# Query and first MLP matrix loaded in one transfer each, as 4.5 rows a partition; 24 rows of the second MLP matrix in one transfer

## The chip, the core and the metric

The kernel runs on one core of a Trainium2 chip. A core has a matrix engine (TensorE, PE in the profile), a vector engine (VectorE, DVE), an activation engine (ScalarE, ACT), a general engine (GpSimd, POOL) and a sync engine (SyncE, SP) that here does little but issue transfers. Each runs its own instructions in program order and waits on semaphores; 16 DMA engines move data between HBM and the on-chip memory. The metric is the device time of one execution in microseconds (us).

## What is computed

One decode step, for a batch of 8 rows x of 576 numbers. Attention reads the last 2048 positions of a cache of 16 key and value heads (32 query heads, 128 wide); beside it an MLP of hidden size 4608 works on the layernormed x; a gate mixes the two.

```python
W = min(4096, max(256, Sk // 4))                  # 2048
q = (x @ wq).reshape(B, Sq, Hq, Dh)               # 576 x 4096
k, v = cache[:, :, Sk - W:, :], repeated for 2 query heads each
o = softmax(q @ k.T * Dh ** -0.5) @ v
a = o.reshape(B, Sq, Hq * Dh) @ wo                # 4096 x 576
y = layernorm(x)
b = gelu(y @ w1 + b1) @ w2 + b2                   # 576 x 4608, 4608 x 576
g = sigmoid((x * gate_w).sum(-1))
return g * a + (1 - g) * b
```

## The kernel before

Nearly all bytes are the cache: 32 transfers of 4 MB (16 of keys, K0 to K15, 16 of values, V0 to V15), each into one of four slots of a large buffer, `RAW`. The slots are taken in the order 1, 2, 0, 3, and the transfers are issued by SP in the order K0, K1, V0, K2, V1, K3, V2 and so on (`stream`, lines 587 to 600). SP issues a transfer when its slot is free (`load_item`, lines 620 to 627, the list `slot_free`): a slot that held keys is free when its last transpose is done (L691), one that held values when its product with the probabilities is done (L754, L186).

The weights of the start lie in slots too. The query matrix `A_wq` goes to slot 0 and the first MLP matrix `B_w1` to slot 3, with a small remainder behind it. So V0 (slot 0) waits for the query matmuls, `o_qp`, and K2 (slot 3) for the MLP matmuls, `o_hp` (line 603).

Rows of the two matrices: 576 = 512 + 64. The first 512 rows lie four to a partition; the last 64 are cut in halves by columns, one half row a partition, so that they fill 128 partitions as well. Each matrix comes in two transfers (lines 417 to 421). A matmul multiplies 128 partitions at once, so there are five steps t over the rows: four for the main part, one for the remainder. The batch is only 8 wide, so four column quarters c of the matrix are multiplied side by side in four 32-column groups of the array (`held_x`, L497 to L505): in step t, a quarter of the output takes 2 matmuls of 512 columns (query) or 3 of 384 (MLP). That makes 5 x 4 x 2 = 40 and 5 x 4 x 3 = 60 matmuls. Those of one step that share their weights follow without a new weight load (line 175).

The transposed input (`xT`, `yT`) has one 128 x 8 block per step. `tr_in` (L448) makes four blocks straight from x with a column step of 4, and two from `xz` (or `yz`), where the last 64 columns are spread to every second place with zeros between, once for each half; `ev_T` copies all six from PSUM in one instruction (L462). DVE also makes the gate (L429, L430), the layernorm (L432 to L439, with a power on POOL, L438) and small masks before the query matmuls.

After the query matmuls: copy (L517), transpose (L522), selection matmuls (L528), four copies on ACT (L537), the mask of the scores (L874). After the MLP matmuls: gelu on ACT and DVE (L556 to L563). Then each key item n takes four transposes on DVE (L691), each followed by 8 matmuls (L709, L175), a maximum (L642), an exponential (L648) and the mask of the next item (L652).

At the end come the bias, the first 24 of 36 rows of `B_w2` in two transfers of 12 (`M_CUTS`, L599), the output matrix in four, and the last 12 rows of `B_w2` in 8, 3 and 1 (`m2_chunk`, L852).

No order is written by hand: a planner, `_Plan.schedule` (L62), orders each engine's work by costs given with each operation.

Of the kernel before, what the change touches and what calls it, by code (L numbers as in the profile page):

```python
# [192 lines left out]
def build_kernel(nc, A_x, A_k_cache, A_v_cache, A_wq, A_wo, B_x, B_w1, B_b1, B_w2, B_b2, gate_w, out):  # L193
# [16 lines left out]
    FCW = 32 * FT  # L210
    HN = 3
    HW_ = FCW // HN
    QCW = Hq * Dh // FC
# [8 lines left out]
    with ExitStack() as es:  # L222
# [34 lines left out]
        req("cols", 16, F32)  # L257
        req("xT", 6 * 32, BF)
        req("yT", 6 * 32, BF)
        req("q4", 4 * 256, BF)  # L260
# [24 lines left out]
        over("y_bf", "PT", 2304, D, BF)  # L285
        over("xz", "PT", 3456, 256, BF)
        over("yz", "PT", 3968, 256, BF)
        over("b1c", "PT", 4608, FCW, BF)
# [37 lines left out]
        cols = view("cols")  # L326
        xT = view("xT").rearrange("p (t b) -> p t b", b=32)
        yT = view("yT").rearrange("p (t b) -> p t b", b=32)
        q4 = view("q4").rearrange("p (h m) -> p h m", h=4)
# [23 lines left out]
        x_sb, gw_sb, y_bf = view("x_sb", 8), view("gw_sb", 8), view("y_bf", 8)  # L353
        xz = view("xz", 8).rearrange("p (s c) -> p s c", s=2)
        yz = view("yz", 8).rearrange("p (s c) -> p s c", s=2)
        xg, xc, sq = view("xg", 8), view("xc", 8), view("sq", 8)
# [4 lines left out]

        wq_m = RAW[:, 0:4 * 4096].rearrange("p (t c) -> p t c", t=4)
        W1O = (ND - 1) * DE
        WQR = W1O + 4 * F + F // 2
        wq_r = RAW[:, WQR:WQR + 2048]
        w1_m = RAW[:, W1O:W1O + 4 * F].rearrange("p (t c) -> p t c", t=4)
        w1_r = RAW[:, W1O + 4 * F:W1O + 4 * F + F // 2]

# [27 lines left out]
        o_nhalf = add("pool", lambda e: e.memset(col(C_NHALF, 8), -0.5), name="nhalf", cost=0.1)  # L396
        o_xz0 = add("pool", lambda e: e.memset(view("xz", 8), 0.0), name="xz0", cost=0.2)
        o_yz0 = add("pool", lambda e: e.memset(view("yz", 8), 0.0), name="yz0", cost=0.2)
        o_z = add("pool", lambda e: e.memset(zeros_bf, 0.0), name="zeros", cost=0.15)
# [16 lines left out]
        db = [d_b1]  # L416
        d_wqr = dma("sp", lambda e: e.dma_start(wq_r, A_wq[512:576, :].rearrange("k (s c) -> (k s) c", s=2)), "wq", 64 * 8192, name="d_wqr")
        d_wqm = dma("sp", lambda e: e.dma_start(wq_m.rearrange("p t c -> p (t c)"), A_wq[0:512, :].rearrange("(p t) c -> p (t c)", t=4)), "wq", 512 * 8192, name="d_wqm", after=[d_wqr])
        dwq = [d_wqm, d_wqr]
        d_w1m = dma("sp", lambda e: e.dma_start(w1_m.rearrange("p t c -> p (t c)"), B_w1[0:512, :].rearrange("(p t) c -> p (t c)", t=4)), "w1", 512 * F * 2, name="d_w1m", after=[d_wqm])  # L420
        d_w1r = dma("sp", lambda e: e.dma_start(w1_r, B_w1[512:576, :].rearrange("k (s c) -> (k s) c", s=2)), "w1", 64 * F * 2, name="d_w1r", after=[d_w1m])
        dw1 = [d_w1m, d_w1r]


        o_xz = []
        for s in range(2):
            o_xz.append(add("dve", (lambda s=s: lambda e: e.tensor_copy(xz[:, s, :].rearrange("p (k z) -> p k z", z=2)[:, :, s], x_sb[:, 512:576]))(),  # L427
                            deps=dx + [o_xz0], name="xz%d" % s, cost=0.12))
        o_xg = add("dve", lambda e: e.tensor_tensor(out=xg, in0=x_sb, in1=gw_sb, op=ALU.mult), deps=dx, name="xg", cost=0.7)  # L429
# [9 lines left out]
        o_y = add("dve", lambda e: e.tensor_scalar(out=y_bf, in0=xc, scalar1=col(C_RSTD, 8), scalar2=None, op0=ALU.mult), deps=[o_rstd, o_xc], name="y", cost=0.4)  # L439
        o_yz = []  # L440
        for s in range(2):
            o_yz.append(add("dve", (lambda s=s: lambda e: e.tensor_copy(yz[:, s, :].rearrange("p (k z) -> p k z", z=2)[:, :, s], y_bf[:, 512:576]))(),
                            deps=[o_y, o_yz0], name="yz%d" % s, cost=0.12))
# [4 lines left out]
        def tr_in(name, z, which):  # L448
            def fn(e):
                ins = None  # L450
                for t in range(4):
                    src = bass.AP(arena, offset=aoffs(name) + t, ap=[[AST, 8], [4, 128]])
                    ins = e.transpose(ps_bf[:, BK_X, which * 64 + t * 8: which * 64 + t * 8 + 8], src, ident[0:8, 0:8])  # L453
                for s in range(2):
# [10 lines left out]
        o_gp = add("pe", lambda e: e.matmul(ps[:, BK_X, 400:402], r8, cols[0:8, C_G:C_G + 2], start=True, stop=True), deps=[o_g, o_omg, o_r8], name="g_pe", cost=0.4, after=[o_yTp])  # L465
        o_yT = add("dve", ev_T(yT, 1), deps=[o_gp, o_yTp, o_yT0], name="yT_ev", cost=0.2)
        o_gcol = add("dve", lambda e: e.tensor_copy(gcol, ps[:, BK_X, 400:401]), deps=[o_gp], name="gcol_ev", cost=0.15)
# [134 lines left out]
        last_dma = [d_w1r]  # L602
        slot_free = [[o_qp], [], [], [o_hp]]
# [248 lines left out]
        def m2_chunk(ci):  # L852
# [95 lines left out]
```

## Time and profile before

| | us |
|---|---|
| median of 3 runs | 364.70 (364.68 to 364.73) |
| the profiled execution, its own time | 364.7 |
| span of the profile, first to last instruction | 363.4 |
| busy: PE, DVE, ACT, POOL | 274.3, 253.9, 131.6, 76.0 |
| moved by DMA | 154.45 MB, mean 425 GB/s |
| mean granted TensorE clock | 0.944 |

The profile page gives busy time by engine, the span in 40 slices, DMA queues, the chain of work that ended last, and groups of instructions by line. Beside the page the trace can be asked for a timeline, for stretches (windows) and for each transfer's time from issue to landing. In a line of the timeline stand the start in us, the length, the engine and line, the operation, what it writes and reads, and how many instructions were merged; in brackets how long its engine had been idle and who released it. A busy TensorE counts pipelined matmuls, so its busy time is no measure of its load.

| issue to landing of the first transfers | issued, us | landed after, us |
|---|---|---|
| query, last 64 rows in halves, 512 KB | 0.81 | 3.4 |
| query, 512 rows, 4096 KB | 1.25 | 12.9 |
| MLP, 512 rows, 4608 KB | 1.72 | 23.4 |
| MLP, last 64 rows in halves, 576 KB | 2.19 | 24.3 |
| K0 | 2.7 | 34.6 |
| V0 | 20.41 | 36.2 |
| K2 | 32.81 | 33.4 |

### The profile page before, as it was taken

What the parts mean: (1) busy time and instruction counts of PE and PEld (TensorE: products, weight loads), DVE (VectorE), ACT (ScalarE), POOL (GpSimd) and SP (SyncE); (2) the same over time, 40 slices, a digit from 0 to 9 for tenths busy, and PEclk for the clock granted to TensorE, in tenths of its full rate; (3) what the DMA queues carried; (4) which work ended last, traced back from release to release, by engine and by line L of the source; (5) the groups of instructions that cost most, each with busy time, mean ns of one, the idle gap of its engine ahead of it and who ended that gap; (6) DMA issues with size and microseconds to landing.
All of it is one profiled execution on the core that took longest, in us unless ns stands there. A gap on an engine that the chain in (4) does not pass through costs nothing.

```text
span 363.4 us, 4421 instructions
## 1 busy us (share of the span) xinstructions
PE 274.3 (75%) x1830; PEld 125.7 (35%) x1382; DVE 253.9 (70%) x196; ACT 131.6 (36%) x117; POOL 76.0 (21%) x76
## 2 busy tenths in 40 slices
PE   0356454999897868895968869786879679988996
PEld 0110000345270605260524316251617034523763
DVE  0722978797978596939486778767695959498520
ACT  1012106274644443543333334444444407313300
POOL 9124001221414040403212040404040403003000
PEclk9975596999999999999999989999989969999999
DMA  8999999999999999999999999999999999999996
GB/s 349 433 422 420 447 418 448 415 451 418 451 415 453 411 458 408 453 411 454 413 451 415 451 415 451 415 451 413 451 418 447 418 447 416 449 418 434 416 425 251
DMA packets 6578, 154.45 MB, mean 425 GB/s; under 512 B 764, under 2 KB 932, under 8 KB 1320
## 3 DMA queue, kind: packets, MB, share of 16 engines
q1 hardware_dynamic: 6512, 154.29, 98.7%
q8 instruction: 6, 0.10, 0.1%
q10 hardware_dynamic: 56, 0.03, 0.0%
q14 instruction: 4, 0.03, 0.0%
HBM read 154.31 MB, written 0.01 MB: 425 GB/s over the span
## 4 chain that ended last, share of the span: by engine, by line
DMA 50%; DVE 33%; PE 9%; issue 4%; ACT 2%; ACTq 0%; POOL 0%; SPq 0%
DMA arena<-in_A_k_cache_dram 43%; DVE arena L691 20%; DMA arena<-in_B_w_dram 5%; DVE arena L666 5%; PE ps L175 4%; DMA arena<-in_gate_w_dram 2%; DVE arena L642 2%; PE ps L186 2%; DVE arena L800 1%; PE ps L502 1%; PE ps L709 1%; DVE arena L797 1%; DVE arena L563 1%; DVE arena L741 1%; ACT arena L648 1%
## 5 line engine op out<-in xcount | busy, mean ns | idle before, releaser
L691 DVE STREAM_TRANSPOSE arena<-arena 128x2048 f32<-128x2048 f32 x64 | 145.0, 2287 | 30.1 <-DMA arena<-in_A_k_cache_dram 28.4
L175 PE MATMUL ps<-arena 128*128 128x512 bf16 (+2 forms) x458 | 127.1, 428 | 11.4 <-DVE arena L691 8.7
L186 PE MATMUL ps<-arena 128*128 x942 | 105.5, 273 | 0.1
L741 POOL COPY arena<-arena 32x2048 bf16<-32x2048 bf16 x28 | 52.7, 1884 | 207.6 <-DVE arena L666 206.8
L186 PEld LDWEIGHTS ps<-arena 128*128 x942 | 91.9, 98 | 11.3 <-issue 0.6
L709 PE MATMUL ps<-arena 128*128 128x512 bf16 x120 | 48.9, 408 | 54.3 <-DVE arena L691 47.6
L740 ACT ACTIVATE arena<-arena 32x2048 bf16<-32x2048 bf16 x30 | 57.2, 1906 | 72.0 <-DVE arena L666 71.7
L709 PEld LDWEIGHTS ps<-arena 128*128 128x128 bf16 x128 | 13.1, 102 | 163.9 <-DVE arena L691 108.6
L648 ACT ACTIVATE arena<-ps,arena 128x2048 bf16<-128x2048 f32 x16 | 31.5, 1967 | 105.2 <-DVE arena L646 72.4
L642 DVE TENSOR_REDUCE arena<-ps 128x1 f32<-128x2048 f32 x16 | 36.7, 2291 | 30.9 <-PE ps L175 30.9
L666 DVE STREAM_TRANSPOSE arena<-arena 128x2048 bf16<-128x2048 bf16 x16 | 36.4, 2274 | 2.1 <-ACT arena L648 2.1
L652 ACT ACTIVATE ps<-arena 128x2048 f32<-128x2048 f32 x15 | 28.1, 1872 | 0.1
L754 PE MATMUL ps<-arena 128*128 128x256 bf16 x82 | 14.3, 272 | 1.0 <-DVE arena L741 1.0
L754 PEld LDWEIGHTS ps<-arena 128*128 128x128 bf16 x82 | 7.8, 98 | 16.1 <-issue 13.7
L453 PE MATMUL ps<-arena 8*128 8x8 bf16 x8 | 0.6, 171 | 14.7 <-DVE arena L427 9.6
L580 PE MATMUL ps<-arena 128*8 128x288 bf16 (+1 forms) x140 | 9.4, 286 | 1.4 <-DMA arena<-in_A_wo_dram 0.7
L558 DVE TENSOR_TENSOR arena<-arena 128x1152 f32<-128x1152 f32 x1 | 1.4, 1358 | 11.1 <-ACT arena L556 11.1
L724 POOL MEMSET arena<- 128x4096 f32 x1 | 3.5, 3511 | 22.6 <-DVE arena L741 22.6
L580 PEld LDWEIGHTS ps<-arena 128*8 128x8 bf16 (+1 forms) x140 | 5.8, 86 | 5.6 <-DMA arena<-in_B_w_dram 1.8
L635 POOL COPY arena<-arena 32x128 bf16<-32x128 bf16 x16 | 4.6, 287 | 14.5 <-ACT arena L537 7.8
L427 DVE COPY arena<-arena 8x64 bf16<-8x64 bf16 x2 | 0.3, 190 | 9.2 <-DMA arena<-in_gate_w_dram 9.2
L891 DVE CAST arena<-ps 8x288 bf16<-8x288 f32 x1 | 0.4, 446 | 8.6 <-PE ps L580 8.6
(104 smaller groups left out, 99.4 us busy)
## 6 DMA issues: line engine op xcount, KB each, us to landing
arena<-in_A_k_cache_dram SPq DMA_DIRECT2D x16, 4096.0 KB, 27.2
arena<-in_A_v_cache_dram SPq DMA_DIRECT2D x16, 4096.0 KB, 27.1
arena<-in_B_w_dram SPq DMA_DIRECT2D x1, 4608.0 KB, 23.4
arena<-in_A_wo_dram SPq DMA_DIRECT2D x4, 1152.0 KB, 22.5
arena<-in_A_wq_dram SPq DMA_DIRECT2D x1, 4096.0 KB, 12.9
arena<-in_B_w_dram SPq DMA_DIRECT2D x2, 1728.0 KB, 23.9
arena<-in_B_w_dram SPq DMA_DIRECT2D x1, 1152.0 KB, 19.8
arena<-in_B_w_dram SPq DMA_DIRECT2D x1, 576.0 KB, 24.3
```

What stands on the lines that cost most here:

```text
L175: return e.add_instruction(mybir.InstMatmult(name=nc.get_next_instruction_name(), engine=mybir.EngineType.PE, ins=[e.lower_ap(rhs), e.lowe ...
L186: return e.add_instruction(mybir.InstMatmult(name=nc.get_next_instruction_name(), engine=mybir.EngineType.PE, ins=[operand(r, r_ap), opera ...
L580: ins = e.matmul(ps[32 * j:32 * j + 8, BK_ACC, 0:JN], lhsT, rhs[:, JN * j:JN * j + JN], start=False, stop=True, skip_group_check=True, til ...
L642: mx = mx_done[n] = add("dve", lambda e: e.tensor_reduce(out=k(n, MX), in_=ps[:, 0:4, :].rearrange("p a n -> p (a n)"), axis=AXL.X, op=ALU ...
L648: ex = add("act", lambda e: e.activation(out=Pm, in_=ps[:, 0:4, :].rearrange("p a n -> p (a n)"), func=ACTF.Exp, bias=k(n, NB), scale=SCAL ...
L652: mask_done[n + 1] = add("act", lambda e: e.activation(out=ps[:, 0:4, :].rearrange("p a (n c) -> p (a n) c", c=32), in_=bass.AP(arena_f, o ...
L666: pt_done[n] = add("dve", lambda e: e.transpose(bass.AP(arena, offset=aoffs("PT") + 2048 * (n % 2), ap=[[AST, 128], [1, 2048]]), Pm), deps ...
L691: tr = add("dve", (lambda rh=rh, hh=hh, kb=kb: lambda e: e.transpose(bass.AP(arena_f, offset=foffs("KT") + kb * 2048, ap=[[AST // 2, 128], ...
L709: mm = e.matmul(*args, start=False, stop=True, skip_group_check=True) if rc == 0 else held_matmul(nc, e, *args, stop=True, skip=True)
L740: return e.activation(out=dst, in_=src, func=ACTF.Copy)
L741: return e.tensor_copy(dst, src)
L754: mm = e.matmul(ps[:, ob_, 0:256], lhsT, rhs, start=(k == 0), stop=True, skip_group_check=True)
```

## The change

The two matrices are seen as 1152 half rows of 2048 (query) or 2304 (MLP) columns. Partition p holds half rows 9p to 9p + 8, which lie together in HBM, so that one transfer of 36,864 or 41,472 bytes a partition loads a whole matrix. The query matrix now begins 4096 bytes ahead of slot 0, in the end of the buffer `KT`, and the MLP matrix ends behind slot 3, in the zone of `ptx0`.

A step i now takes the i-th half row of each partition. For even p + i that is a left half, for odd p + i a right half, of row (9p + i) // 2. So the input of a step is spread over the partitions (`rows_of`: two strided copies of 8 x 640, one for even and one for odd steps), transposed (nine transposes for each of x and y), and written to `xT` or `yT` twice, once masked by even and once by odd parity (`ev_T`: a product with the columns of `par`, two instructions each). The column quarters 0 and 1 use the blocks masked for left halves, 2 and 3 those for right halves. There are nine steps in place of five: 72 matmuls for 40 (query) and 108 for 60 (MLP). `xr` is shared by x and y, so the copies of y wait for the transposes of x. `par` is two small instructions on DVE from the identity matrix; the zeroed `xz` and `yz` and the four copies into them are gone, and the memsets of `xT` and `yT` on POOL cover 576 elements in place of 192.

The first 24 rows of `B_w2` come in one transfer. Their matmuls stay in two groups of 12, in the same order, both waiting for that transfer.

```diff
+    HR = 2 * D // 128
...
-        wq_m = RAW[:, 0:4 * 4096].rearrange("p (t c) -> p t c", t=4)
-        W1O = (ND - 1) * DE
-        WQR = W1O + 4 * F + F // 2
-        wq_r = RAW[:, WQR:WQR + 2048]
-        w1_m = RAW[:, W1O:W1O + 4 * F].rearrange("p (t c) -> p t c", t=4)
-        w1_r = RAW[:, W1O + 4 * F:W1O + 4 * F + F // 2]
+        QH, FH = Hq * Dh // 2, F // 2
+        WQO, W1O = aoffs("RAW") - (HR * QH - DE), aoffs("RAW") + (ND - 1) * DE
+        assert WQO >= aoffs("KT") + 6144 and W1O + HR * FH <= PX + SE
+        wq_sb = arena[:, WQO:WQO + HR * QH].rearrange("p (i c) -> p i c", i=HR)
+        w1_sb = arena[:, W1O:W1O + HR * FH].rearrange("p (i c) -> p i c", i=HR)
...
-        d_wqr = dma("sp", lambda e: e.dma_start(wq_r, A_wq[512:576, :].rearrange("k (s c) -> (k s) c", s=2)), "wq", 64 * 8192, name="d_wqr")
-        d_wqm = dma("sp", lambda e: e.dma_start(wq_m.rearrange("p t c -> p (t c)"), A_wq[0:512, :].rearrange("(p t) c -> p (t c)", t=4)), "wq", 512 * 8192, name="d_wqm", after=[d_wqr])
-        dwq = [d_wqm, d_wqr]
-        d_w1m = dma("sp", lambda e: e.dma_start(w1_m.rearrange("p t c -> p (t c)"), B_w1[0:512, :].rearrange("(p t) c -> p (t c)", t=4)), "w1", 512 * F * 2, name="d_w1m", after=[d_wqm])
-        d_w1r = dma("sp", lambda e: e.dma_start(w1_r, B_w1[512:576, :].rearrange("k (s c) -> (k s) c", s=2)), "w1", 64 * F * 2, name="d_w1r", after=[d_w1m])
-        dw1 = [d_w1m, d_w1r]
-
-
-        o_xz = []
-        for s in range(2):
-            o_xz.append(add("dve", (lambda s=s: lambda e: e.tensor_copy(xz[:, s, :].rearrange("p (k z) -> p k z", z=2)[:, :, s], x_sb[:, 512:576]))(),
-                            deps=dx + [o_xz0], name="xz%d" % s, cost=0.12))
+        half_rows = lambda w: w.rearrange("k (s c) -> (k s) c", s=2).rearrange("(p i) c -> p (i c)", i=HR)
+        d_wq = dma("sp", lambda e: e.dma_start(wq_sb.rearrange("p i c -> p (i c)"), half_rows(A_wq)), "wq", D * 8192, name="d_wq")
+        d_w1 = dma("sp", lambda e: e.dma_start(w1_sb.rearrange("p i c -> p (i c)"), half_rows(B_w1)), "w1", D * F * 2, name="d_w1", after=[d_wq])
+        dwq, dw1 = [d_wq], [d_w1]
...
+        o_par01 = add("dve", lambda e: e.tensor_reduce(out=par[:, 0:2], in_=ident.rearrange("p (k h) -> p h k", h=2), axis=AXL.X, op=ALU.add), deps=[o_ident], name="par01", cost=0.3, prio=1)
+        o_par = add("dve", lambda e: e.tensor_copy(par[:, 2:3], par[:, 0:1]), deps=[o_par01], name="par2", cost=0.12, prio=1)
+
+        def rows_of(name, odd):
+            def fn(e):
+                dst = bass.AP(arena, offset=aoffs("xr") + 128 - 127 * odd, ap=[[AST, 8], [256, (HR + 1) // 2], [128, 2], [2, 64]])
+                src = bass.AP(arena, offset=aoffs(name) + HR // 2 * odd, ap=[[AST, 8], [1, (HR + 1) // 2], [0, 2], [HR, 64]])
+                return e.tensor_copy(dst, src)
+            return fn
+
+        def tr_in(which):
             def fn(e):
                 ins = None
-                for t in range(4):
-                    src = bass.AP(arena, offset=aoffs(name) + t, ap=[[AST, 8], [4, 128]])
-                    ins = e.transpose(ps_bf[:, BK_X, which * 64 + t * 8: which * 64 + t * 8 + 8], src, ident[0:8, 0:8])
-                for s in range(2):
-                    ins = e.transpose(ps_bf[:, BK_X, which * 64 + 32 + s * 8: which * 64 + 40 + s * 8], z[:, s, :], ident[0:8, 0:8])
+                for i in range(HR):
+                    ins = e.transpose(ps_bf[:, BK_X, which * 128 + i * 8: which * 128 + i * 8 + 8], xr[:, i + 1, :], ident[0:8, 0:8])
                 return ins
             return fn
 
-        o_xTp = add("pe", tr_in("x_sb", xz, 0), deps=dx + o_xz + [o_ident], name="xT_pe", cost=0.6)
-
-        def ev_T(dst, which):
-            return lambda e: e.tensor_copy(dst[:, :, 0:8], ps_bf[:, BK_X, which * 64: which * 64 + 48].rearrange("p (t b) -> p t b", b=8))
-        o_xT = add("dve", ev_T(xT, 0), deps=[o_xTp, o_xT0], name="xT_ev", cost=0.2)
-        o_yTp = add("pe", tr_in("y_bf", yz, 1), deps=[o_y, o_ident, o_xT] + o_yz, name="yT_pe", cost=0.6)
+        o_xr = [add("dve", rows_of("x_sb", odd), deps=dx, name="xr%d" % odd, cost=0.7) for odd in range(2)]
+        o_xTp = add("pe", tr_in(0), deps=o_xr + [o_ident], name="xT_pe", cost=0.9)
+
+        def ev_T(which, odd):
+            def fn(e):
+                n = (HR + 1 - odd) // 2
+                dst = bass.AP(arena, offset=aoffs("xy"[which] + "T") + 64 * odd, ap=[[AST, 128], [128, n], [32, 2], [1, 8]])
+                src = bass.AP(ps_bf, offset=BK_X * 1024 + which * 128 + 8 * odd, ap=[[2 * PST, 128], [16, n], [0, 2], [1, 8]])
+                return e.tensor_tensor(out=dst, in0=src, in1=bass.AP(arena_f, offset=foffs("par") + odd, ap=[[AST // 2, 128], [0, n], [1, 2], [0, 8]]), op=ALU.mult)
+            return fn
+        o_xTe = add("dve", ev_T(0, 0), deps=[o_xTp, o_xT0, o_par], name="xT_ev0", cost=0.2)
+        o_xT = add("dve", ev_T(0, 1), deps=[o_xTe], name="xT_ev1", cost=0.2)
+        o_yr = [add("dve", rows_of("y_bf", odd), deps=[o_y, o_xTp], name="yr%d" % odd, cost=0.7) for odd in range(2)]
+        o_yTp = add("pe", tr_in(1), deps=o_yr + [o_ident, o_xT], name="yT_pe", cost=0.9)
         o_gp = add("pe", lambda e: e.matmul(ps[:, BK_X, 400:402], r8, cols[0:8, C_G:C_G + 2], start=True, stop=True), deps=[o_g, o_omg, o_r8], name="g_pe", cost=0.4, after=[o_yTp])
-        o_yT = add("dve", ev_T(yT, 1), deps=[o_gp, o_yTp, o_yT0], name="yT_ev", cost=0.2)
+        o_yTe = add("dve", ev_T(1, 0), deps=[o_gp, o_yTp, o_yT0, o_par], name="yT_ev0", cost=0.2)
+        o_yT = add("dve", ev_T(1, 1), deps=[o_yTe], name="yT_ev1", cost=0.2)
...
-            for t in range(5):
+            for t in range(HR):
                 def rhs_of(t, c, i):
-                    if t < 4:
-                        return wq_m[:, t, QCW * c + 512 * i:QCW * c + 512 * i + 512]
-                    return wq_r[:, QCW * (c % 2) + 512 * i:QCW * (c % 2) + 512 * i + 512]
-                ins = held_x(e, lambda c, i: ps[32 * c:32 * c + 32, BK_Q + i, :], lambda t, c: xT[:, t if t < 4 else 4 + c // 2, :], rhs_of, 2, t, t == 0, t == 4)
+                    return wq_sb[:, t, QCW * (c % 2) + 512 * i:QCW * (c % 2) + 512 * i + 512]
+                ins = held_x(e, lambda c, i: ps[32 * c:32 * c + 32, BK_Q + i, :], lambda t, c: xT[:, t, c // 2, :], rhs_of, 2, t, t == 0, t == HR - 1)
...
-            for t in range(5):
+            for t in range(HR):
                 def rhs_of(t, c, i):
-                    if t < 4:
-                        return w1_m[:, t, FCW * c + HW_ * i:FCW * c + HW_ * i + HW_]
-                    return w1_r[:, FCW * (c % 2) + HW_ * i:FCW * (c % 2) + HW_ * i + HW_]
-                ins = held_x(e, lambda c, i: ps[32 * c:32 * c + 32, BK_H + i, 0:HW_], lambda t, c: yT[:, t if t < 4 else 4 + c // 2, :], rhs_of, HN, t, False, t == 4)
+                    return w1_sb[:, t, FCW * (c % 2) + HW_ * i:FCW * (c % 2) + HW_ * i + HW_]
+                ins = held_x(e, lambda c, i: ps[32 * c:32 * c + 32, BK_H + i, 0:HW_], lambda t, c: yT[:, t, c // 2, :], rhs_of, HN, t, False, t == HR - 1)
...
-        M_CUTS = [[12, 12], [8, 3, 1]]
+        M_CUTS = [[24], [8, 3, 1]]
...
-                ops.append(AccGroup("m2_%d_%d" % (ci, n), mms, [o_hT, d], cost=0.16 * jn, after=o_m2[-1:] + ([us_done[NG - 1]] if ci == 0 and n else [])).op)
-                o_m2.append(ops[-1])
+                for k0 in range(0, jn, 12):
+                    ops.append(AccGroup("m2_%d_%d" % (ci, n + k0), mms[k0:k0 + 12], [o_hT, d], cost=0.16 * len(mms[k0:k0 + 12]), after=o_m2[-1:] + ([us_done[NG - 1]] if k0 else [])).op)
+                    o_m2.append(ops[-1])
```

More of the change, by code (lines that the diff above doesn't have):

```diff
@@ L257, in build_kernel @@
         req("cols", 16, F32)
-        req("xT", 6 * 32, BF)
-        req("yT", 6 * 32, BF)
+        req("par", 3, F32)
+        req("xT", 2 * HR * 32, BF)
+        req("yT", 2 * HR * 32, BF)
         req("q4", 4 * 256, BF)
@@ L285, in build_kernel @@
         over("y_bf", "PT", 2304, D, BF)
-        over("xz", "PT", 3456, 256, BF)
-        over("yz", "PT", 3968, 256, BF)
+        over("xr", "KT", 8704, (HR + 2) * 128, BF)
         over("b1c", "PT", 4608, FCW, BF)
@@ L326, in build_kernel @@
         cols = view("cols")
-        xT = view("xT").rearrange("p (t b) -> p t b", b=32)
-        yT = view("yT").rearrange("p (t b) -> p t b", b=32)
+        xT = view("xT").rearrange("p (i h b) -> p i h b", h=2, b=32)
+        yT = view("yT").rearrange("p (i h b) -> p i h b", h=2, b=32)
+        par = view("par")
+        xr = view("xr", 8).rearrange("p (i c) -> p i c", c=128)
         q4 = view("q4").rearrange("p (h m) -> p h m", h=4)
@@ L353, in build_kernel @@
         x_sb, gw_sb, y_bf = view("x_sb", 8), view("gw_sb", 8), view("y_bf", 8)
-        xz = view("xz", 8).rearrange("p (s c) -> p s c", s=2)
-        yz = view("yz", 8).rearrange("p (s c) -> p s c", s=2)
         xg, xc, sq = view("xg", 8), view("xc", 8), view("sq", 8)
@@ L396, in build_kernel @@
         o_nhalf = add("pool", lambda e: e.memset(col(C_NHALF, 8), -0.5), name="nhalf", cost=0.1)
-        o_xz0 = add("pool", lambda e: e.memset(view("xz", 8), 0.0), name="xz0", cost=0.2)
-        o_yz0 = add("pool", lambda e: e.memset(view("yz", 8), 0.0), name="yz0", cost=0.2)
         o_z = add("pool", lambda e: e.memset(zeros_bf, 0.0), name="zeros", cost=0.15)
@@ L439, in build_kernel @@
         o_y = add("dve", lambda e: e.tensor_scalar(out=y_bf, in0=xc, scalar1=col(C_RSTD, 8), scalar2=None, op0=ALU.mult), deps=[o_rstd, o_xc], name="y", cost=0.4)
-        o_yz = []
-        for s in range(2):
-            o_yz.append(add("dve", (lambda s=s: lambda e: e.tensor_copy(yz[:, s, :].rearrange("p (k z) -> p k z", z=2)[:, :, s], y_bf[:, 512:576]))(),
-                            deps=[o_y, o_yz0], name="yz%d" % s, cost=0.12))
         o_g = add("dve", lambda e: e.tensor_scalar(out=col(C_G, 8), in0=col(C_T, 8), scalar1=0.5, scalar2=0.5, op0=ALU.mult, op1=ALU.add), deps=[o_t], name="g", cost=0.12)
@@ L446, in build_kernel @@
         o_dgb = add("dve", lambda e: e.tensor_scalar(out=dg[:, 8:16], in0=idf8, scalar1=col(C_OMG, 8), scalar2=None, op0=ALU.mult), deps=[o_omg, o_idf], name="dgb", cost=0.12)
-        def tr_in(name, z, which):
+        o_par01 = add("dve", lambda e: e.tensor_reduce(out=par[:, 0:2], in_=ident.rearrange("p (k h) -> p h k", h=2), axis=AXL.X, op=ALU.add), deps=[o_ident], name="par01", cost=0.3, prio=1)
+        o_par = add("dve", lambda e: e.tensor_copy(par[:, 2:3], par[:, 0:1]), deps=[o_par01], name="par2", cost=0.12, prio=1)
@@ L454, in fn @@
-                for s in range(2):
-                    ins = e.transpose(ps_bf[:, BK_X, which * 64 + 32 + s * 8: which * 64 + 40 + s * 8], z[:, s, :], ident[0:8, 0:8])
-                return ins
-            return fn
-        o_xTp = add("pe", tr_in("x_sb", xz, 0), deps=dx + o_xz + [o_ident], name="xT_pe", cost=0.6)
-        def ev_T(dst, which):
-            return lambda e: e.tensor_copy(dst[:, :, 0:8], ps_bf[:, BK_X, which * 64: which * 64 + 48].rearrange("p (t b) -> p t b", b=8))
-        o_xT = add("dve", ev_T(xT, 0), deps=[o_xTp, o_xT0], name="xT_ev", cost=0.2)
@@ L598, in regs @@
             return held_regs
-        M_CUTS = [[12, 12], [8, 3, 1]]
+        M_CUTS = [[24], [8, 3, 1]]
         stream += [("B", 0), ("M", 0), ("W", 0), ("M", 1)]
-        last_dma = [d_w1r]
+        last_dma = [d_w1]
         slot_free = [[o_qp], [], [], [o_hp]]
```

## The prediction

> **What bounds the kernel now.** I first read the page's row of DMA load in 40 slices:
>
> ```profile
> DMA  8999999999999999999999999999999999999996
> GB/s 349 433 422 420 447 418 448 415 451 418 451 415 453 411 458 408 453 411 454 413 451 415 451 415 451 415 451 413 451 418 447 418 447 416 449 418 434 416 425 251
> ```
>
> The 16 DMA engines are loaded from the second slice to the last but one, at 425 GB/s on average, while no compute engine passes 75% of the span. The time is 154 MB over that rate plus a start and a tail. No computation costs anything until it lets the transfer queue run dry; a gap in the queue is never made up. So the question is how near the queue comes to running dry, and that stands in the order in which SP issues the transfers (start, length, line):
>
> ```profile
> 2.66 1.25 SPq L624 DMA_DIRECT2D arena<-in_A_k_cache_dram  x2
> 20.41 0.54 SPq L624 DMA_DIRECT2D arena<-in_A_v_cache_dram  x1
> 32.81 0.54 SPq L624 DMA_DIRECT2D arena<-in_A_k_cache_dram  x1
> 50.67 0.53 SPq L624 DMA_DIRECT2D arena<-in_A_v_cache_dram  x1
> 67.89 0.53 SPq L624 DMA_DIRECT2D arena<-in_A_k_cache_dram  x1
> 76.91 0.54 SPq L624 DMA_DIRECT2D arena<-in_A_v_cache_dram  x1
> ```
>
> These are K0 and K1, then V0, K2, V1, K3, V2, each 4.19 MB. V0 waits for the query matmuls (slot 0 held their matrix), K2 for the MLP matmuls (slot 3), V1 and K3 for the transposes of K0 and K1. The DMA view gives the time from issue to landing of the first query transfer, of V1 and of K3 (last number):
>
> ```profile
> arena<-in_A_wq_dram SPq DMA_DIRECT2D x1, 512.0 KB, 3.4
> ...
> arena<-in_A_v_cache_dram SPq DMA_DIRECT2D x1, 4096.0 KB, 25.2
> ...
> arena<-in_A_k_cache_dram SPq DMA_DIRECT2D x1, 4096.0 KB, 17.7
> ```
>
> V1 lands at 50.67 + 25.2 = 75.9 and K3 at 67.89 + 17.7 = 85.6, one transfer later (9.7 us, as 4.19 MB / 430 GB/s says). How long would K3 take with nothing ahead of it? The first transfer of the program had nothing ahead: 3.4 us, of which 0.52 MB / 430 GB/s = 1.2 is data and 2.2 is not. So K3 alone needs 2.2 + 9.7 = 11.9, and stood 17.7 - 11.9 = 5.8 us in the queue. A second count: query, MLP and five cache transfers are 31.0 MB, which the windows of the trace reach at 74.0; K3's rows could flow about 0.9 after its issue, at 68.8: 5.2. I take 5.5 us. That is the smallest **lead** of the kernel (V2 18.3, K4 21.1, V3 22.1, later 25 to 27 us to landing), so what delays K3's issue by more than 5.5 us makes the kernel longer by the excess.
>
> What sets K3's issue is one chain without slack; the timeline and the chain of waits show its joints:
>
> ```profile
> 1.75 7.38 DMA arena<-in_gate_w_dram
> ...
> 9.16 0.29 DVE arena L427 x2
> ```
> ```profile
> 15.56 0.56 PE L465 MATMUL ps<-arena 8*128 8x2 f32 x2
> 16.05 0.62 PE L502 MATMUL ps<-arena 128*32 128x512 bf16 x4
> 16.45 0.64 PE L175 MATMUL ps<-arena 128*32 128x512 bf16 x4
> ...
> 22.98 0.61 PE L528 MATMUL ps<-arena 128*128 128x256 bf16 x4 [2.61 <-DVE arena L522]
> ...
> 25.30 1.49 PE L175 MATMUL ps<-arena 128*128 128x512 bf16 x3 [1.71 <-ACT arena L537]
> ...
> 30.95 0.85 PE L175 MATMUL ps<-arena 128*32 128x384 bf16 x8
> ...
> 31.91 0.85 PE L175 MATMUL ps<-arena 128*32 128x384 bf16 x8
> ...
> 32.81 1.13 ACT L556 ACTIVATE arena<-ps 128x1152 f32<-128x1152 f32 x1 [5.79 <-PE ps L175]
> ...
> 38.27 2.30 DVE L691 STREAM_TRANSPOSE arena<-arena 128x2048 f32<-128x2048 f32 x1
> ...
> 65.55 2.31 DVE L691 STREAM_TRANSPOSE arena<-arena 128x2048 f32<-128x2048 f32 x1 [0.29 <-PE ps L175]
> ```
>
> The gate row lands at 9.13; DVE makes the gate, the layernorm and the transposed inputs; the query matmuls start at 16.12, behind the y transposes and the gate matmul in TensorE's order, and end at 20.39; copy, transpose, select and mask follow to 26.8; the MLP matmuls end at 32.81; DVE does u2, w and v before K0's first transpose at 38.27, though K0 had landed at 2.7 + 34.6 = 37.3. From there DVE, then QK, max, exp, mask and QK again, run back to back to K1's last transpose, which ends at 67.86 and releases K3.
>
> **The change part by part, as delay D of K3's issue.**
>
> *Transfers.* Two rows of SP fewer at the start (0.39 and 0.43 of issue), bytes unchanged. The gate row now queues behind 36 KB rows from the first moment, where it met eight 4 KB rows and then 32 KB ones; quarter-us windows show 16 such rows ending every 1.25 us, five times between 3.5 and 9.0. Five rows times 1.25 times one eighth is 0.8, and the small rows before them cost less than one big one. I take +0.65, bounds 0 (it meets as many bytes) to 1.4 (one more row).
>
> *DVE.* The two small copies (0.29 together) become four copies of 640 elements with a step of 9 at the source. None like it is in the trace. Nearest from below: a 576-element tensor_scalar, 0.51, so perhaps 0.41; from above: the strided transpose L563, 2.30 for 1152, 2.0 ns an element, so 1.3. A 576-element multiply takes 0.66 to the next, 0.75 for 640: I take 0.75. One runs under the pow on GpSimd (0.73 from its input to L439); three and its excess lie on the chain, 2.35. The parity-masked evictions of x (two, 0.14 each) and three 8x8 ops that stood under the pow (0.3) now stand between y and its transposes; gone are the small copies and one eviction (0.4). Net +2.2 (bounds 1.1 to 4.4). The parity columns are made before 9 us, when DVE is idle; the larger memsets on GpSimd end before 9 too.
>
> *TensorE.* Nine transposes of y for six: 3 x 0.06 = +0.18. Query: 72 matmuls for 40; four take 0.427 (16.05 to 16.45 and on, ten groups to 20.39): 32 x 0.107 = **+3.41**. MLP: 108 for 60; twelve take 0.96 (30.95 to 31.91): 48 x 0.080 = **+3.82**. All lie on the chain. One discount: after the query matmuls L528 ran four 256-column matmuls in 0.61, twice the rate of the mask matmuls (three of 512 in 1.49). So the clock rises late in a busy stretch, and longer stretches may see some of it. No group within either stretch of the trace is quicker, so 0 is one bound; the other is the two added parts at 64 ns a matmul (what L580's 72 take with their weight loads, 4.58 us): 1.4 + 0.8 = 2.2. I take -1.1.
>
> Sum: 0.65 + 2.2 + 0.18 + 3.41 + 3.82 - 1.1 = 9.2 us. V0 is then issued at about 26 and K2 at 42, both covered (the queue holds work to 54.4 by the windows' bytes); V1 at 59.9, where K2's bytes end near 64: covered. K3 at 77.1 is not: 9.2 - 5.5 = **3.7 us of empty queue**. Work behind it: V2 comes 9.0 after K3's issue while K3 itself takes 9.7, then K4 15.9 after against two transfers (19.4). So the queue stays fed from there and the lead grows again; the gap is paid once.
>
> *Second MLP matrix.* One transfer of 24 rows for two of 12: the two landed at 341.9 and 345.9, and the first matmul on them stands at 348.78. The merged one lands with the second, 2.9 us ahead: 0; if the cover were gone, 24 matmuls (1.5 us) would slide behind the next group. SP saves one issue, in a queue 17 us deep.
>
> The profiled execution spans 363.4 and took 364.7, 1.3 around it, which is the median of the runs. 363.4 + 3.7 + 1.3 = 368.4.
>
> **The rivals.**
>
> *A: the lead covers it.* TensorE goes at twice the rate through the later part of both stretches. For it: L528. Against: 0.50 is the granted clock through the whole MLP stretch, which had been busy since 25.3, and the last query group is no faster than the first. Price: half of what lies beyond the first 3.4 us of each, (7.68 - 3.4)/2 + (8.64 - 3.4)/2 = 4.8 saved in place of 1.1, D = 5.5: it decides from there on. Then only the transfers count: the 0.5 MB of 4 KB rows that end at 3.5 us cost perhaps 0.3 against the mean rate, 24 to 28 us (410 GB/s, with 4.6 KB rows, against 430) 0.2: 364.2. The Trainium skill, "TensorE: Matmul & The Clock Gate", Part 1: The HAM clock gate, speaks for it: the clock doubles after some 3.4 us of sustained work; the stretch of the MLP in this trace does not agree.
>
> *B: more delay.* Strided copies at 1.3 us each (+2.2), or the gate row one row later (+0.75), or no discount (+1.1): D of 10.3 to 13, 369.5 to 372. For it: L563's rate. Against: a plain copy is not a transpose.
>
> *C: a second gap.* V2's margin is 9.7 - 9.0 = 0.7 us. If PV of the first item starts later, up to 1 us more: 369.4. Against: it follows K1's QK as before.
>
> *D: the merge pays by itself* (fewer, longer rows raise the rate). Against: 9 KB rows of the output matrix run at 424 to 432 GB/s, 32 KB ones at 430. The Trainium skill, "DMA: Bandwidth & Descriptors", Rules for kernel authors, asks for coalescing into transfers of 1 MiB and more. By it three removed sub-transfers could gain something near 1 us; the rows bear out only the 0.5 of A.
>
> **How the numbers follow.** My forecast 0.63, A 0.13, B 0.15, C 0.06, D 0.03. A measurement tells 0.2% (0.7 us) from no change. Slower: forecast, B and C, 0.84. A gives mostly "same", D faster: same 0.09, faster 0.07. The forecast alone has D between 7 and 11, 366 to 370. The range reaches toward A below and into B above: 364.9 to 371.0, leaving out A's lower part and B's tail.
>
> **What would show it.** A gap in the DMA row of the changed profile in the slices around 74 to 79 us; query matmuls from about 19 to 26; MLP ending near 42; K3 issued near 77 and landing 11.9 later; V2 and all later lead times longer again. The gate row landing at 9.8; four copies of 0.75. Wrong would be: K3's issue before 73.4 (no gap), spread copies far from 0.75 us, or a gap elsewhere.

## The result, and the profile after

| | before | after |
|---|---|---|
| median of 5 runs, us | 364.73 (364.68 to 364.92) | 370.81 (369.93 to 371.73) |
| profiled execution, us | 364.7 | 369.93 |
| its span, us | 363.4 | 368.7 |
| moved by DMA | 154.45 MB, mean 425 GB/s | 154.47 MB, mean 419 GB/s |
| DMA packets | 6578 | 6147 |

The ratio is 1.017, with a 95% interval of 1.0152 to 1.0188: the changed kernel is slower by 6.1 us. Its profiled execution is the fastest of its five; there the span grew by 5.3. Its page shows the same load of the DMA engines as before but for one slice:

```profile
DMA  8999999969999999999999999999999999999995
GB/s 322 463 416 432 420 448 413 444 224 411 437 441 423 437 437 427 436 428 434 441 420 441 430 432 441 420 437 441 423 441 427 436 441 417 441 430 430 421 422 237
```

The ninth slice (73.7 to 83.0 us) moves 224 GB/s. Windows of that place (start and end, length, busy time of the engines, granted clock, share of the DMA engines, GB/s) show where:

```profile
74.00:77.00 3.00, 2.33 (x10) 0.19 (x2) 2.31 (x1) 0.19 (x1) 0.21 (x1) 1.00 0.08 33
77.00:78.00 1.00, 1.00 (x6) 0.10 (x1) 0.00 (x0) 0.00 (x0) 0.00 (x0) 1.00 0.64 164
78.00:79.00 1.00, 1.00 (x9) 0.64 (x7) 0.40 (x1) 0.00 (x0) 0.00 (x0) 1.00 1.22 328
79.00:80.00 1.00, 1.00 (x11) 0.90 (x10) 1.00 (x1) 0.00 (x0) 0.00 (x0) 1.00 0.32 131
```

Next to nothing moves for about three microseconds, and the restart is slow: between 77 and 79 the engines are busy 1.86 us (0.64 + 1.22) for 0.49 MB, which is 15 rows of 32 KB at 2.0 us each on 16 engines. In a full queue a row takes 1.2 (a share of 0.99 for 426 GB/s). Why it runs dry stands in SP's issues (V0, K2, V1, K3, V2) and in the times from issue to landing of K3 and V2:

```profile
27.43 0.54 SPq L624 DMA_DIRECT2D arena<-in_A_v_cache_dram  x1
41.34 0.53 SPq L624 DMA_DIRECT2D arena<-in_A_k_cache_dram  x1
59.20 0.53 SPq L624 DMA_DIRECT2D arena<-in_A_v_cache_dram  x1
76.56 0.54 SPq L624 DMA_DIRECT2D arena<-in_A_k_cache_dram  x1
85.58 0.54 SPq L624 DMA_DIRECT2D arena<-in_A_v_cache_dram  x1
```
```profile
arena<-in_A_k_cache_dram SPq DMA_DIRECT2D x1, 4096.0 KB, 12.9
...
arena<-in_A_v_cache_dram SPq DMA_DIRECT2D x1, 4096.0 KB, 15.1
```

The bytes of V1 had run out by 74.5; K3 was issued at 76.56, in place of 67.89. It lands at 89.5 (85.6 before), V2 at 100.7 (95.2 before). From there the lag stays: 5.5 us at V2's landing, 5.3 at the end.

The chain in front of K3 has grown on DVE (start, length, line):

```profile
10.04 0.75 DVE L421 TENSOR_TENSOR arena<-arena 8x576 f32<-8x576 bf16 x1 [7.83 <-DMA arena<-in_gate_w_dram]
...
12.09 1.30 DVE L443 COPY arena<-arena 8x640 bf16<-8x640 bf16 x1
...
15.50 1.30 DVE L443 COPY arena<-arena 8x640 bf16<-8x640 bf16 x1
...
17.76 1.30 DVE L443 COPY arena<-arena 8x640 bf16<-8x640 bf16 x1
...
19.11 1.30 DVE L443 COPY arena<-arena 8x640 bf16<-8x640 bf16 x1
```

and on TensorE, where the query matmuls run from 21.22 to 27.4 and the MLP matmuls from 34.40 to 41.34:

```profile
21.22 0.62 PE L506 MATMUL ps<-arena 128*32 128x512 bf16 x4
21.62 0.64 PE L175 MATMUL ps<-arena 128*32 128x512 bf16 x4
...
25.93 0.38 PE L506 MATMUL ps<-arena 128*32 128x512 bf16 x4
26.15 0.38 PE L175 MATMUL ps<-arena 128*32 128x512 bf16 x4
...
38.54 0.82 PE L175 MATMUL ps<-arena 128*32 128x384 bf16 x8
...
40.81 0.49 PE L175 MATMUL ps<-arena 128*32 128x384 bf16 x8
```

These lines are to be read by their starts: four query matmuls take 0.43 us up to 25.5 and 0.215 from there, 12 MLP matmuls 0.96 up to 39.2 and 0.49 from there. The rate doubles in the midst of each stretch.

### The profile page after: what moved, and what is told of

The parts are those of the page before. It is cut to its first block, busy times and chain, and to the rows that moved or that the text cites. A ratio compares the mean times of both kernels' runs of the same rounds, so it can differ in the third digit from the quotient of the medians.

```text
span 368.7 us, 4542 instructions
## 1 busy us (share of the span) xinstructions
PE 279.4 (76%) x1916; PEld 126.7 (34%) x1420; DVE 259.1 (70%) x200; ACT 131.6 (36%) x117; POOL 76.2 (21%) x74
## 2 busy tenths in 40 slices
DMA packets 6147, 154.47 MB, mean 419 GB/s; under 512 B 716, under 2 KB 884, under 8 KB 1016
## 4 chain that ended last, share of the span: by engine, by line
DMA 49%; DVE 34%; PE 10%; issue 4%; ACT 2%; ACTq 0%; SPq 0%
DMA arena<-in_A_k_cache_dram 41%; DVE arena L691 19%; DMA arena<-in_B_w_dram 5%; DVE arena L666 5%; PE ps L175 5%; DMA arena<-in_gate_w_dram 2%; DVE arena L642 2%; PE ps L186 2%; PE ps L506 1%; DVE arena L443 1%; DVE arena L800 1%; PE ps L709 1%; DVE arena L797 1%; DVE arena L563 1%; DVE arena L741 1%
## 5 line engine op out<-in xcount | busy, mean ns | idle before, releaser
L175 PE MATMUL ps<-arena 128*128 128x512 bf16 (+2 forms) x506 | 131.8, 423 | 11.2 <-DVE arena L691 8.7
L186 PEld LDWEIGHTS ps<-arena 128*128 x942 | 92.0, 98 | 11.2 <-issue 0.6
L580 PE MATMUL ps<-arena 128*8 128x288 bf16 (+1 forms) x140 | 9.4, 286 | 1.4 <-DMA arena<-in_A_wo_dram 0.7
L506 PE MATMUL ps<-arena 128*32 128x512 bf16 (+1 forms) x72 | 8.8, 478 | 0.0
L539 ACT ACTIVATE arena<-ps 128x256 bf16<-128x256 f32 x4 | 1.2, 388 | 18.3 <-PE ps L530 18.3
L580 PEld LDWEIGHTS ps<-arena 128*8 128x8 bf16 (+1 forms) x140 | 5.8, 86 | 5.6 <-DMA arena<-in_B_w_dram 1.9
```

The lines of the kernel that those rows point to most:

```text
L175: return e.add_instruction(mybir.InstMatmult(name=nc.get_next_instruction_name(), engine=mybir.EngineType.PE, ins=[e.lower_ap(rhs), e.lowe ...
L186: return e.add_instruction(mybir.InstMatmult(name=nc.get_next_instruction_name(), engine=mybir.EngineType.PE, ins=[operand(r, r_ap), opera ...
L580: ins = e.matmul(ps[32 * j:32 * j + 8, BK_ACC, 0:JN], lhsT, rhs[:, JN * j:JN * j + JN], start=False, stop=True, skip_group_check=True, til ...
```

## The experiments

The edits are shortened; words in brackets stand for the lines left out. The brackets behind a ratio are its 95% interval, and each time is compared with that of the kernel before in the same session.

**Parts of the change alone.** The first has nothing but the merged rows of the second MLP matrix (with the split of their matmuls into two groups, as in the change):

```diff
-        M_CUTS = [[12, 12], [8, 3, 1]]
+        M_CUTS = [[24], [8, 3, 1]]
```

> The kernel before with one part of the change: 24 rows of the second MLP matrix in one transfer. Theory 1 (the cost is the queue running dry ahead of K3): no change, 364.7 within 0.3, since the merged transfer lands with the old second one, near 346, ahead of the matmuls at 348.8. Rival (the tail pays: the first 12 rows arrive 4 us later and their matmuls slide): up to +1.5 us, and the first matmuls on the matrix start after 348.8.

364.98 against 364.93, ratio 1.0001 (0.9991 to 1.001). The merged transfer, issued at 319.8, landed 27.2 us later, at 347.0, ahead of the first matmuls on it, which now start at 349.11. It costs and gains nothing.

The second has the two merged transfers alone, with the five steps of before:

```diff
-        d_wqr, d_wqm, d_w1m, d_w1r = (the four transfers of before)
+        d_wq = dma("sp", ..., half_rows(A_wq), "wq", ...)
+        d_w1 = dma("sp", ..., half_rows(B_w1), "w1", ..., after=[d_wq])
```

> The kernel before with the query and first MLP matrix in one transfer each, in the changed places, but the five steps, the operands and the matmuls of before; the steps read the first five half rows of each partition, so the product is another one. Theory 1: the gate row lands near 10.0, the delay of K3's issue is about 1 us, no gap, and the time is 364.0 to 364.8 (nothing, or at most 0.6 us from fewer and longer rows). Rival (the merged transfers themselves are the cost, by their long rows): above 367.

365.00, ratio 1.0002 (0.9993 to 1.0012). The gate row landed at 10.36 (9.16 before), K3 was issued at 68.39, half a us late, and no gap opened. No byte is won either: up to 40 us 16.3 MB are moved in both kernels.

The third has the rest: nine steps, spread operands and masks, but four transfers.

```diff
-        d_wq, d_w1 = (one transfer each)
+        d_wqr = dma(..., wq_sb[:, 8], A_wq[512:576] in halves)
+        d_wqm = dma(..., wq_sb[:, 0:8], A_wq[0:512], four rows a partition)
+        (the same for B_w1)
```

> The changed kernel, but the two matrices come in four transfers as before, put into the changed places one after the other, so that each row holds another part of the matrix and the product is another one; operands, masks and matmuls are those of the change. Theory 1: the gate row lands near 9.1 again, K3's issue is 7.5 to 9 us later than before, and the time is 368.5 to 370.5, nearly all of the loss. Rival (the transfers are the cost): back to 364.7 within 0.7.

369.28, ratio 1.0123 (1.01 to 1.0145). Gate row at 9.26, K3 at 75.93, span 368.0. So the transfers cost 0 alone, and about 2 us where the computing has already eaten the lead (369.28 against 370.81 in the first result, 371.63 in the next run): the parts of this change do not add up, since the first few microseconds of delay are nearly free.

**The changed kernel again**, unaltered.

> The changed kernel once more, for a second profile. The five runs shown spread over 1.8 us where those of before spread over 0.24. Theory 1 with the clock as its reason: the query and MLP stretches end earlier or later by up to 1.7 us each, as the rise of the clock falls into them early or late; K3's issue and the span move together by that amount, and the time is 369.9 to 371.8. Rival (the spread lies in the DMA engines or behind K3): K3's issue within 0.2 of 76.56 whatever the span.

371.63 (370.97 to 372.49); profiled span 370.3, K3 at 78.35. K3 and the span moved together, by 1.8 and 1.6 us, but the reason given was mostly wrong for this pair. The two matmul stretches were longer by 0.4 each, and the selection and mask between them shorter by 0.4; the rest came in at the start:

```profile
11.30 0.75 DVE L421 TENSOR_TENSOR arena<-arena 8x576 f32<-8x576 bf16 x1 [9.08 <-DMA arena<-in_gate_w_dram]
```

The gate row landed 1.26 us later than in the first profile, about one 36 KB row of the matrix on a DMA engine (in quarter-us windows such rows end some 1.35 apart). In the five profiles with four transfers there it landed at 9.12 to 9.53, in the five with the two merged ones (and the gate row in two transfers of ACT's) at 9.97, 10.04, 10.36, 11.30 and 11.38.

**The delay without the change.** The kernel before, with the copy of the query result done several times more on DVE:

```diff
+        held_back = []
+        for k in range(3):   # 7 in the other run
+            held_back.append(add("dve", (the copy of q_sb), deps=[o_qp, o_ssq, o_y] + held_back[-1:]))
```

> The kernel before with the copy of the query result done three times more on DVE (3 x 1.24 = 3.7 us on the chain to K3, nothing else). Theory 1 with a lead of 4.8 us (K3 alone took 12.9 from issue to landing in the changed kernel, and 17.7 with the queue ahead of it): no loss, 364.7 within 0.4. Rival (no lead, every us of the chain counts): 368.4.

> The kernel before with that copy done seven times more (7 x 1.24 = 8.7 us on the chain to K3, the delay that the changed kernel had in its profile). Theory 1: a gap in the DMA row ahead of K3 and 8.7 - 4.8 = 3.9 us, and up to 1.4 for the slow restart that the changed kernel showed: 368.6 to 370.1, the same loss as the change with none of its parts. Rival (the loss is in the parts of the change, not in the delay): 364.7 within 0.5. Rival (every us counts): 373.4.

Three copies: 365.52, ratio 1.0013 (1.0004 to 1.0022), K3 3.2 us late. Seven copies: 369.16, ratio 1.0121 (1.0106 to 1.0135), K3 7.6 us late, span 367.4. Of the 8.8 us that the copies add, 1.4 are won back as the matmuls became quick earlier in this run (query stretch 3.8 us for 4.4, MLP 4.1 for 5.0), 0.6 behind K2's issue, and 0.8 are added by the later gate row and slower selection. The copies in the trace of the second, and the gap:

```profile
20.26 8.78 DVE L519 CAST arena<-ps 128x1024 bf16<-128x1024 f32 x7 [3.34 <-PE ps L175]
```
```profile
74.00:75.00 1.00, 1.00 (x6) 0.10 (x1) 1.00 (x1) 0.00 (x0) 0.00 (x0) 1.00 0.16 66
75.00:76.00 1.00, 0.78 (x5) 0.10 (x1) 0.46 (x1) 0.00 (x0) 0.00 (x0) 1.00 0.00 0
```

A delay of the size of the change, with none of its parts, costs most of what the change costs; a delay of 3.2 us costs half a microsecond, where none had been expected: the lead is smaller than the 4.8 us assumed for these two runs.

**Shorter chains in the changed kernel.** First, TensorE kept busy with 24, 11, 10 and 5 matmuls on zeros ahead of the x transposes, the y transposes, the selection and the mask:

```diff
+        def warm_up(name, n, first, then, banks):
+            ... n matmuls of 512 columns, zeros_bf by maskR, start=True
+        warm_up("warm_a", 24, [o_acc0], o_xTp, (2, 3))
+        warm_up("warm_b", 11, [o_xTp], o_yTp, (2, 3))
+        warm_up("warm_c", 10, [o_qp], o_selp, (2, 3))
+        warm_up("warm_d", 5, [o_selp], o_mask0, (4, 5))
```

> The changed kernel with TensorE kept busy by idle matmuls on zeros ahead of the x and y transposes, behind the query matmuls and ahead of the mask, in banks that hold nothing then. Theory 1 with the clock: all query groups take 0.214 and all MLP steps 0.49, the stretches take 3.9 and 4.4 for 6.13 and 6.9, the mask 0.9 for 1.27, so K3's issue comes near 71.5, 3.6 after before, under the lead: no gap, 364.2 to 365.2. Rival (matmuls in four column groups are held by something else than the clock): 370 to 371.

The timeline has every query group at the quick rate:

```profile
20.96 0.40 PE L506 MATMUL ps<-arena 128*32 128x512 bf16 x4
21.18 0.39 PE L175 MATMUL ps<-arena 128*32 128x512 bf16 x4
```

The stretch takes 4.1 us, that of the MLP 4.6, K3 is issued at 70.60, no gap, and the profiled execution, the fastest of the six, took 364.93. The median is 366.42 (364.93 to 368.83), above what was expected, ratio 1.0052 (1.0032 to 1.0073). So the clock's part is shown for that execution; the spread is wider than a gate row one row late explains (K3 then 4.0 us late, a loss of 0.6), and what the slowest of these runs met was not profiled and stays open.

Second, three of the four spreading copies on ACT:

```diff
-        o_xr = [add("dve", rows_of("x_sb", odd), ...) for odd in range(2)]
+        o_xr = [add("act", rows_of("x_sb", odd, True), ...) for odd in range(2)]
-        o_yr = [add("dve", rows_of("y_bf", odd), ...) for odd in range(2)]
+        o_yr = [add(("dve", "act")[odd], rows_of("y_bf", odd, odd == 1), ...) for odd in range(2)]
```

> The changed kernel with the two spreading copies of x and one of y moved from DVE (1.30 each) to ACT, which waits there. Theory 1: the x copies leave the chain (2 x 1.30 less the 0.7 that lay under the pow) and one of y runs beside the other (1.30): K3's issue comes 3 us earlier, near 73.5, and of a loss of 6.1 about 3 remain: 367 to 368.5. Rival (the loss does not hang on the chain): 370.8.

368.32, ratio 1.0084 (1.0069 to 1.0098). From gate row to query matmuls 8.0 us in place of 11.2: the 3 us are there. But the gate row landed at 11.38 in this profile, and from the query matmuls to the end of the MLP the chain took 1.2 us longer than in the changed kernel (21.3 for 20.1; the selection matmuls 1.04 for 0.61), so K3 stood at 75.87 and not near 73.5.

Third and fourth, the gate row in one transfer, and x and the gate row issued by SP ahead of the matrices:

```diff
-                       for r0, r1 in ((0, 6), (6, 8))]
+                       for r0, r1 in ((0, 8),)]          # one run
-        d_x, d_gw, d_gw1 = dma("act", ...)
+        d_x, d_gw, d_gw1 = dma("sp", ...), ahead of d_wq  # the other run
```

> The changed kernel with the gate row alone in one transfer. Theory: each small transfer on ACT's queue waits behind two big rows of the matrix on its DMA engine, so one transfer fewer brings the gate row 2.4 to 2.7 us earlier, near 7.5, K3's issue near 74.0, and the time to 367.5 to 368.7. Rival (the gate row waits for a fixed count of big rows, whatever stands ahead of it): gate row at 10.0 or 11.3, 370 to 372.

> The changed kernel with x and the gate row issued by SP ahead of the query matrix. Theory: the gate row lands near 4, the query matmuls then wait for their matrix (about 15.5) and no longer for DVE, K3's issue comes 2.5 to 3.5 after that of before, at the edge of the lead; all transfers start about 1 us later: 365.5 to 366.7. Rival (the loss lies in the longer matmul stretches whatever starts them): above 368.

One transfer: 368.94, ratio 1.0122 (1.0107 to 1.0138), K3 at 75.31. The gate row came one big row earlier, not two:

```profile
8.81 0.85 DVE L421 TENSOR_TENSOR arena<-arena 8x576 f32<-8x576 bf16 x1 [6.60 <-DMA arena<-in_gate_w_dram]
```

It does hang on what stands ahead of it, but the price of a small transfer was taken twice too high. Issued first: 366.55, ratio 1.0043 (1.0026 to 1.0061); the query matmuls start at 15.7, but their stretch takes 6.9 us (6.2 in the changed kernel, 4.4 before) and that of the MLP 6.9, and K3 is issued 4.7 us late. The six times lie in two groups, three at 365.8 and three at 367.3 to 367.6; the profile is one of the second, and what parts them stays open.

Last, all helps together (zeros, ACT, one gate transfer):

> The changed kernel with three helps at once: TensorE kept busy as in the run before, the copies on ACT, and the gate row in one transfer of 8 partitions in place of 6 and 2. Theory as the runs so far have mended it (loss = delay of K3's issue less a lead of 3.4 us): K3's issue is no later than before, so no loss and no spread: 364.6 to 365.2, the time of before, and no gain either, since the merged transfers alone changed nothing. Rival (merged transfers gain once the gap is gone): below 364.3.

364.88 (364.76 to 365.02), ratio 1.0001 (0.9992 to 1.001). K3 is issued 0.8 us late and stands in the queue again:

```profile
68.73 0.53 SPq L638 DMA_DIRECT2D arena<-in_A_k_cache_dram  x1
```
```profile
arena<-in_A_k_cache_dram SPq DMA_DIRECT2D x1, 4096.0 KB, 17.1
```

With the gap closed and the changed transfers in place, nothing is won: no version came out ahead of the kernel before.

**All profiles in one table**, times in us; the delay is K3's issue less 67.89.

| kernel | gate row | K3's issue | delay | span less 363.4 | delay less the span's growth |
|---|---|---|---|---|---|
| changed | 10.04 | 76.56 | 8.67 | 5.3 | 3.4 |
| changed, again | 11.30 | 78.35 | 10.46 | 6.9 | 3.6 |
| computing only | 9.26 | 75.93 | 8.04 | 4.6 | 3.4 |
| copies on ACT | 11.38 | 75.87 | 7.98 | 4.7 | 3.3 |
| seven copies more | 9.53 | 75.49 | 7.60 | 4.0 | 3.6 |
| gate in one | 8.81 | 75.31 | 7.42 | 3.9 | 3.5 |
| gate row first | 3.08 | 72.54 | 4.65 | 2.6 | 2.1 |
| three copies more | 9.12 | 71.08 | 3.19 | 0.9 | - |
| zeros | 9.97 | 70.60 | 2.71 | 0.3 | - |
| all helps | 8.74 | 68.73 | 0.84 | 0.3 | - |
| transfers only | 10.36 | 68.39 | 0.50 | 0.2 | - |
| second MLP matrix only | 9.13 | 67.41 | -0.48 | 0.4 | - |

Six profiles, of five kernels with quite different edits, share one line: what the delay has beyond 3.3 to 3.6 us is lost. The line is good to some 0.5 us: the last row, whose start is untouched, has its K3 0.48 early, and in the later sessions the kernel before spanned 363.6 to 363.7 and not 363.4. It is no sharp edge either, as three copies cost 0.9 of span below it. The kernel with the gate row first does not lie on it. All its transfers begin later (V0 lands at 57.64, for 56.61 before), which takes 1.0 us; the rest of its 2.6 is more than the line allows and is not explained.

## Why the prediction was right, and where it was off

Right were the mechanism, its place and its sign: the queue runs dry ahead of K3, once, at 74 us, because K3's issue hangs on a chain without slack from the gate row on; K2 and V1 are covered; the second MLP matrix costs nothing. Two sums were off. In the delay the errors cancelled: DVE was 2.0 us dearer than taken and the matmul stretches 2.4 cheaper, so that 9.2 came close to 8.67 by luck. In the lead nothing cancelled, and the forecast of 368.4 was 2.4 short. 370.81 lies beyond the 366 to 370 of the forecast alone and 0.2 inside the stated range, whose upper end came from rival B; the repeated kernel, 371.63, lies outside it.

| term, us | predicted | first profile | from |
|---|---|---|---|
| gate row | +0.65 | +0.88 | 9.16, 10.04 |
| DVE, gate row to y transposes | +2.2 | +4.23 | 6.19, 10.42 |
| TensorE, transposes and gate | +0.18 | +0.06 | 0.70, 0.76 |
| query matmuls | +3.41 | +1.85 | 4.36, 6.21 |
| from there to the MLP matmuls | 0 | -0.40 | 7.37, 6.97 |
| MLP matmuls | +3.82 | +1.91 | 5.03, 6.94 |
| clock | -1.1 | within the rows above | |
| to K3's issue | 0 | +0.14 | 35.08, 35.22 |
| delay | 9.2 | 8.67 | |
| lead | 5.5 | 3.4 | |
| loss | 3.7 | 5.3 | |

*The spreading copies* took 1.30 us each, the upper bound, and I had taken 0.75 from contiguous rows. By the prediction's own list, copies far from 0.75 were a sign of being wrong, and that sign came; rival B had priced them right. The nearest row was the other one, L563, with its 2.0 ns an element: its source steps too. Here 640 elements at 1.30 are 2.0 ns as well, and on ACT one takes 1.3 to 1.4. The term was also added up wrongly: its parts (2.35, 0.28 and 0.3 less 0.4) make 2.5 and not 2.2. The Trainium skill, "SBUF — State Buffer", section Door 1: The DMA port swizzle, has the rule: full rate needs two accesses to each 16-byte line. By it a step of 18 bytes, which puts each element into another line, is slow; the trace agrees as far as 2.0 ns an element go against the 1.3 of the multiply of 576 neighbours (0.75 us, L421), but no run has the same copy without the step.

*The clock.* Rival A's mechanism was real. I had bounded the quick rate by 64 ns a matmul, from L580; the quick groups take 54 (0.215 / 4) and 41 (0.49 / 12), so the rise saved 3.5 us (3.41 + 3.82 less 1.85 + 1.91) where 1.1 was taken. Against it the prediction held that no query group of the kernel before was quicker; but its last one is in part, 0.50 us long where the others are 0.64:

```profile
19.44 0.64 PE L502 MATMUL ps<-arena 128*32 128x512 bf16 x4
19.87 0.50 PE L175 MATMUL ps<-arena 128*32 128x512 bf16 x4
```

Rival A was priced at 4.8 saved against a lead of 5.5. With the copies as dear as they were, the rise would have had to save 5.3 more than it did (8.67 less 3.4) to reach the true lead. Only the runs with zeros get there.

*The lead* was the step that mattered most. It was read as "K3 alone takes 2.2 + 9.7", with the 2.2 from the first transfer of the program, 4 KB rows. K3 alone took 12.9 in four of the six profiles with a gap (13.0 and 14.4 in the others): 3.2 that is not data. And rival C had seen that V2 might fall behind, but thought of a late issue. V2 was issued 9.02 after K3 in every kernel; yet in the changed one it landed 11.2 after K3 and not 9.6. So the dry queue costs 1.0 at K3 and 1.6 more at V2: 5.8 as first counted, less 2.6, is 3.2. How it is shared between the two differs (with the computing only, K3 took 14.4 and V2 landed 9.5 behind it), so the lead is better read at V2. Its time from issue to landing before the change was

```profile
arena<-in_A_v_cache_dram SPq DMA_DIRECT2D x1, 4096.0 KB, 18.3
```

and 14.4 to 15.1 in the six profiles with a gap, which leaves 3.2 to 3.9. The count of 5.2 by bytes did not know of this. Why a dry queue restarts slowly, no run shows.

*The spread* of the changed kernel (1.8 us over five runs, 0.24 before) was not foreseen. Before, what comes late at the start is covered by the lead; without a lead it is seen at the end. A later gate row accounts for most of the step from the first profile to the second (1.26 of the 1.8 us of K3's issue). It is not the whole of the spread: computing only and the seven copies spread by 1.8 and 1.5 us over four runs, with the four transfers with which the gate row landed within 0.4 us in all five profiles. The query and MLP stretches differ by up to 0.9 us between profiles of kernels that have them alike (3.8 to 4.5, and 4.1 to 5.0), which is a second cause; how much each has in the median of 6.1 was not measured.

*Rival D*, that merging pays by itself: refuted by the transfers alone (1.0002) and by the kernel with all helps (1.0001).

## What to carry to other kernels

Where the DMA queue is full from end to end, a change off the path costs nothing until it makes one transfer's issue later than the queue's lead at that point; find the smallest lead in the times from issue to landing, and compare each delay with it and not with zero. Take the lead from the landing of the transfers behind as well, since a queue that ran dry restarts slowly. A merge of large transfers that lengthens the computing behind them has nothing to gain where, as here, the bytes moved by a given time are the same without it (16.3 MB at 40 us).

## What was not expected of the hardware

- Two small transfers of ACT's queue land with the big rows of SP's: with 36 KB rows from the start the gate row lands at 9.97 to 11.38, against 9.12 to 9.53; one small transfer fewer brings it about one row (1.23 us) earlier.
- After a dry queue the first 15 rows of 32 KB took 2.0 us each on their DMA engines, for 1.2 in a full queue, and the transfer behind landed 11.2 us after the first, although it was issued 0.7 us earlier than the usual pace of 9.7 asks.
- The granted clock changes on a grid. In the first 60 us of all thirteen profiles the distances between its changes are multiples of 3.4 us, to 0.15 (changed kernel: 32.3, 39.1, 46.0, 52.8; kernel before: 23.5, 43.9, 57.6). So a stretch becomes quick by where it lies on that grid and not a fixed time after its start. By the rate of its matmuls, the query stretch does so 3.0 us (seven copies) to 5.7 us (gate row first) after its start, the MLP stretch of the changed kernel 4.8 us after, and that of the kernel before not at all in its 5.0. That slow stretch was therefore no evidence against rival A. How busy such an interval of 3.4 us has to be was not tested.
